# Decay factors of a Mamba-2 scan made once per row and spread from device memory; last stores on two queues

## Chip, cores and metric

The kernel runs on one core of a Trainium2 chip. The metric is the device time of one launch in microseconds (us). Engines: PE (matrix products), DVE (vector), ACT (scalar, activation), POOL (general, elementwise here), SP (here only a queue that issues transfers). SP's and ACT's queues both issue DMA transfers.

## What is computed

A state-space scan (Mamba-2) over 4 batches, 8 heads, 768 steps, head width 32, state width 16, and then a two-layer network with a PReLU between.

```python
log_a = np.log(np.clip(a, 1e-06, 1.0))
for c in range(nc):                      # chunks of the sequence
    cum = np.cumsum(log_a[:, :, sl], axis=-1)
    L = np.exp(cum[:, :, :, None] - cum[:, :, None, :]) * causal
    y_intra = einsum('bhij,bhjd->bhid', einsum('bhin,bhjn->bhij', Cc, Bc) * L, xc)
    y_inter = einsum('bhin,bhnd->bhid', Cc, state) * np.exp(cum)[:, :, :, None]
    y[:, :, sl] = y_intra + y_inter
    state = exp(sum(la)) * state + sum_j Bc[j] xc[j] * exp(cum[-1] - cum[j])
x = y.transpose(0, 2, 1, 3).reshape(3072, 256)
h = x @ w_in                             # 256 x 2048
g = np.maximum(h, 0) + alpha * np.minimum(h, 0)
out = g @ w_out                          # 2048 x 256
```

The result does not depend on the length of a chunk. The kernel takes chunks of 128 steps instead of 32, and products of the factors instead of exponentials of sums of logarithms.

## The kernel before

**Pairs.** The sequence has 24 chunks of 128 steps, 6 to a batch. Two chunks form a pair, so there are pairs 0 to 11. `load_pair` issues a pair's transfers on SP: `ap`, the decay factors `a` of 8 heads, each on 16 partitions; `nat`, the rows of B and C; `xt`, the rows of x; and from pair 2 on two tiles `abc` of 128 x 1024, in which every partition holds the factors of all 8 heads of one chunk. For pairs 0 and 1 PE spreads the factors instead (`spread`).

**One pair's work** (`pair`, a generator that is advanced in stages). `pair_loads` clamps both `abc` on POOL (L295) to 1e-6 ... 1, puts 0 at the first step of each head (L297), and then makes `bn` (L302): the rows of B times the decay from their step to the chunk's end. That decay, `prt`, comes from `rows_scan`, a backward scan over 96 rows (2 batches x 8 heads x 6 chunks) on DVE (L269 to L273), and from `rows_turn`, which transposes it on PE (L281). `rows_scan` is made for batches 0 and 1 at pair 0 and for batches 2 and 3 at pair 6. DVE clamps `ap` (L359) and scans it forward into `pf` (L362, two scans of 128), the decay from the chunk's start. `pf` scales C to `cd` (L384) and the old state (L406). `decays` scans `abc` against a repeated identity into `dec`, the matrix L (L340, 128 x 1024; L345 for pairs 0 and 1). PE makes B's product with x (L397, from `bn`), the Gram matrix (L422), and from `dec` the output y (L436, L443), which ACT copies to `xT`.

**The network.** `hidden` multiplies `xT` by a piece of w_in (L465); ACT and DVE apply the PReLU (L468, L469; DVE's result is `gt`). The first 512 tokens go through it in halves of 256 and through `output` (L478) while the weights arrive. Weights come in 16 pieces of 512 KB (`raw`, L171), of 64-bit floats that ACT, POOL and DVE convert (L187 to L218). Afterwards come five groups of 512 tokens, with `hidden_sums` (L513: four subtractions on POOL per 256 hidden units), `products` (L528: seven products in place of eight), `combine` and `finish`, which transposes two tiles on DVE (L559) and stores each in four transfers (L562). `weight_sums` (L501) on POOL runs during the first of these groups.

**Order.** It is written out by hand: the program's order on each engine is the order of the calls, each engine works through its own list, and a semaphore holds an instruction until its inputs are there. Each engine and each queue is strictly in order, SP's too: a transfer that waits for its buffer holds the ones behind it. `abc` has three buffers, so a pair's second `abc` load waits on SP until the pair before has ended its first scan. Transfers take turns on eight semaphores, so each also waits for the eighth before it.

Of the kernel before, what the change touches and what calls it, by code (L numbers as in the profile page):

```python
# [12 lines left out]
ALU = mybir.AluOpType  # L13
# [9 lines left out]
def kernel(  # L23
# [62 lines left out]
    xtp = ctx.enter_context(tc.tile_pool(name="xtp", bufs=2))  # L86
    gp = ctx.enter_context(tc.tile_pool(name="gp", bufs=16))
    op = ctx.enter_context(tc.tile_pool(name="op", bufs=2))
    ps_s = ctx.enter_context(tc.tile_pool(name="ps_s", bufs=2, space=PSUM))
    ps_h = ctx.enter_context(tc.tile_pool(name="ps_h", bufs=2, space=PSUM))  # L90
    ps_q = ctx.enter_context(tc.tile_pool(name="ps_q", bufs=1, space=PSUM))
# [18 lines left out]
    def load_rows(i):  # L110
# [2 lines left out]
        nc.sync.dma_start(out=rows, in_=a.rearrange("b h (c t) -> (b h c) t", t=Q)[i * RW : (i + 1) * RW])  # L113
        loads["r", i] = rows

    def load_pair(gp):

        b, c = divmod(2 * gp, CPB)
        sl = slice(c * Q, (c + 2) * Q)
        nat = ldx.tile([P, 2, 2, H * N], F32, name="nat")  # L120
        xt = ldx.tile([P, 2, HD], F32, name="xt")
        ap = ldx.tile([P, 2 * Q], F32, name="ap")
        first = a[b, 0:1, sl]
        nc.sync.dma_start(out=ap, in_=bass.AP(tensor=first.tensor, offset=first.offset,
                                              ap=[[S, H], [0, N], [1, 2 * Q]]))
# [12 lines left out]
        for k in range(2 if gp >= NB else 0):  # L138
            t = lda.tile([P, H * Q], F32, name="abc")
            first = a[b, 0:1, slice((c + k) * Q, (c + k + 1) * Q)]  # L140
            nc.sync.dma_start(
                out=t.rearrange("p (h t) -> p h t", h=H),
                in_=bass.AP(tensor=first.tensor, offset=first.offset, ap=[[0, P], [S, H], [1, Q]]),
            )
            abc.append(t)
        loads["p", gp] = nat, abc, xt, ap

# [114 lines left out]
    masked = {}  # L262
    prt = {}

    def rows_scan(i):
# [7 lines left out]
        nc.vector.tensor_tensor_scan(out=pr[:, ::-1], data0=d0[:, 1:][:, ::-1],  # L273
                                     data1=ends[:RW, ::-1], initial=0.0,
                                     op0=ALU.mult, op1=ALU.add)
        return pr

    def rows_turn(i, pr):

        ps = ss_tile()  # L280
        nc.tensor.transpose(ps[:, :RW], pr, ident[:RW, :RW])  # L281
        if i == 0:
            nc.tensor.transpose(ps[:, RW : RW + NF], al_n, ident[:NF, :NF])
        t = bat.tile([P, RW], F32, name="prt")
        nc.scalar.copy(out=t, in_=ps[:, :RW])
        if i == 0:
            nc.scalar.copy(out=alpha, in_=ps[:, RW : RW + NF])
        prt[i] = t

    def pair_loads(gp):  # L290

        b, c = divmod(2 * gp, CPB)
        nat, abc, xt, ap = loads["p", gp]
        for t in abc:
            nc.gpsimd.tensor_scalar(out=t, in0=t, scalar1=1.0, scalar2=1e-6,  # L295
                                    op0=ALU.min, op1=ALU.max)
            nc.gpsimd.memset(t[:, ::Q], 0.0)  # L297

        bn = work.tile([P, 2, H * N], F32, name="bn")
        i, bi = divmod(b, 2)  # L300
        pj = prt[i].rearrange("p (b h c) -> p b c h", b=2, h=H)[:, bi, c : c + 2]
        nc.gpsimd.tensor_tensor(  # L302
            out=bn.rearrange("p k (h n) -> p k h n", h=H),
            in0=nat[:, 0].rearrange("p k (h n) -> p k h n", h=H),
            in1=pj.unsqueeze(3).to_broadcast([P, 2, H, N]), op=ALU.mult)
        return bn
# [22 lines left out]
    def pair(gp):  # L329
# [21 lines left out]
        if gp == 0:  # L351
            ahead[0] = spread(z, 0)
            rows_turn(0, rows_scan(0))
        elif gp == 6:
            rows_turn(1, rows_scan(1))
        bn = pair_loads(gp)

        pf = work.tile([P, 2 * Q], F32, name="pf")
        nc.vector.tensor_scalar(out=ap, in0=ap, scalar1=1e-6, scalar2=1.0, op0=ALU.max, op1=ALU.min)  # L359
        for k in range(2):  # L360
            ks = slice(k * Q, (k + 1) * Q)
            nc.vector.tensor_tensor_scan(out=pf[:, ks], data0=ap[:, ks], data1=zeros, initial=1.0,  # L362
                                         op0=ALU.mult, op1=ALU.add)
        if gp == 0:
            decays(0)

# [188 lines left out]
    def finish(g):  # L555

        for i, c in enumerate(ends_of.pop(g)):
            o = op.tile([P, GT], F32, name="o_sb")
            nc.vector.transpose(o, c.rearrange("p h t -> p (h t)"))  # L559
            for a4 in range(P // 32):  # L560
                m0 = i * HM + 32 * a4
                nc.sync.dma_start(  # L562
                    out=out[g * GT : (g + 1) * GT, m0 : m0 + 32].rearrange("(b r) c -> r b c", r=32),
                    in_=o[32 * a4 : 32 * a4 + 32].rearrange("r (b c) -> r b c", c=32))

# [26 lines left out]
    for n in range(2):  # L592
        for f in range(NF):
            i = (n * NF + f) // 2
            if (n, f) in ((0, 9), (1, 1), (1, 9)):
                load_pair({(0, 9): 2, (1, 1): 3, (1, 9): 4}[n, f])
            if f in (first, second)[n]:
                ssm(*(first, second)[n][f])
            if f % 2 == 0 and i + 2 < len(pieces):
                convert_a(*pieces[i + 2])  # L600
            hidden(0, f, n * 2 * Q, 2 * Q)
            if f % 2 == 0:
                if i + 6 < len(pieces):
# [8 lines left out]
    for i in range(NQ * (NG - 1) + LAG):  # L612
        g, q = divmod(NQ + i, NQ)
        nxt = 2 * g + 2 + q // 4
        if q % 4 == 0 and nxt < NP:
            if nxt == 4:
                load_rows(1)
            if nxt + 1 < NP:
                load_pair(nxt + 1)
        if i < NQ:  # L620
# [47 lines left out]
```

## Time and profile before

| | |
|---|---|
| median of 3 runs | 435.44 us (435.26 to 435.72) |
| profiled execution, whole | 437.33 us |
| its span, first to last instruction | 435.6 us |
| mean granted PE clock | 0.978 |
| busy: PE, DVE, ACT, POOL | 402.2, 237.6, 123.2, 246.7 us |
| POOL clamps L295 | 20 of 1658 ns, 33.2 us |
| DVE scans L362 | 24 of 772 ns, 17.6 us |
| DVE clamps L359 | 12 of 524 ns, 6.3 us |

Times are from the profiled execution. A row of a timeline reads: start in us, length in us, engine, line, operation, output and inputs, shapes, and in brackets how long the engine had stood idle before and what released it. "x4" are four such instructions. A row of the chain of waits has only start, length, engine, tile and line. "PEclk" or the granted clock is the share of full speed that PE had. The stages: start to about 107 us (weights arrive, pairs 0 to 3 are scanned, the first 512 tokens), then the loop over five groups of 512 tokens to about 420 us, two pairs to a group, then the end.

### The profile page before, as it was taken

To read this page: it belongs to the slowest core of one execution; us is meant where nothing else is said; L and a number is where in the kernel's file an instruction comes from. 1 tells how busy PE (TensorE), PEld (TensorE's weight loads), DVE (VectorE), ACT (ScalarE), POOL (GpSimd) and SP (SyncE) were. 2 spreads that over 40 slices of the span, in tenths; PEclk is the share of its full clock that TensorE was granted. 3 is DMA by queue.
4 is the path that set the end of the run, shared out by engine and by line. 5 is a ranking of instruction groups with operands and counts; after the bars stand their busy time and mean duration, and the time that the engine had idled before them with its cause. 6 is when DMAs were issued, how large, how long until landed. Compare 5 with 4: busy or idle time off the path is not lost.

```text
span 435.6 us, 5196 instructions
## 1 busy us (share of the span) xinstructions
PE 402.2 (92%) x1851; PEld 262.9 (60%) x1851; DVE 237.6 (55%) x347; ACT 123.2 (28%) x236; POOL 246.7 (57%) x306
## 2 busy tenths in 40 slices
PE   5877699999999798999899899899899899999992
PEld 4564548778566455656557557556557556666671
DVE  5999796772834633954832853842853842252223
ACT  3554713523223111313212312312312312131210
POOL 2345676371786955953943953953953942453441
PEclk9998969999999899999999999999999999999997
DMA  9949775250530610105730105730102000002002
GB/s 217 233 159 203 229 187 96 70 93 0 132 74 1 123 35 0 50 1 88 155 73 2 48 0 85 157 74 2 48 1 50 0 0 2 0 8 43 0 0 48
DMA packets 123609, 30.32 MB, mean 70 GB/s; under 512 B 96752, under 2 KB 119488, under 8 KB 123584
## 3 DMA queue, kind: packets, MB, share of 16 engines
q1 hardware_dynamic: 119424, 29.74, 30.4%
q10 hardware_dynamic: 4160, 0.26, 0.6%
q8 instruction: 14, 0.23, 0.2%
q14 instruction: 11, 0.09, 0.1%
HBM read 26.85 MB, written 3.15 MB: 69 GB/s over the span
## 4 chain that ended last, share of the span: by engine, by line
PE 76%; POOL 13%; DVE 7%; issue 1%; DMA 1%; ACT 1%; DVEq 0%; POOLq 0%; ACTq 0%
PE hp L465 32%; PE bank L528 23%; PE bank L478 6%; POOL abc L295 6%; PE ss L422 5%; POOL gt L513 3%; PE ss L443 2%; PE ss L436 2%; PE ss L397 2%; DVE dec L345 2%; DVE wr L215 1%; POOL bn L302 1%; PE ss L371 1%; DVE gt L469 1%; DMA ap<-in_a_dram 1%
## 5 line engine op out<-in xcount | busy, mean ns | idle before, releaser
L513 POOL TENSOR_TENSOR gt<-gt 128x256 f32<-128x256 f32 x160 | 134.6, 854 | 128.7 <-DVE gt L469 109.7
L465 PE MATMUL hp<-xT,w_in 128*128 128x512 f32 (+1 forms) x416 | 182.2, 561 | 2.3 <-DVE gt L469 2.3
L469 DVE SCALAR_TENSOR_TENSOR gt<-hp,s_mul,gt 128x512 f32<-128x512 f32 (+1 forms) x104 | 71.4, 687 | 147.6 <-ACT gt L468 147.1
L468 ACT ACTIVATE gt<-hp,s_alpha 128x512 f32<-128x512 f32 (+1 forms) x104 | 66.6, 641 | 233.4 <-PE hp L465 204.0
L465 PEld LDWEIGHTS hp<-xT,w_in 128*128 128x128 f32 x416 | 77.2, 194 | 65.4 <-issue 53.7
L528 PEld LDWEIGHTS bank<-gt,w_out 128*128 128x128 f32 x320 | 61.0, 191 | 41.2 <-issue 36.7
L528 PE MATMUL bank<-gt,w_out 128*128 128x256 f32 x320 | 82.2, 379 | 0.0
L528 PE MATMUL bank<-gt,ws 128*128 128x256 f32 x240 | 64.9, 379 | 0.0
L340 DVE TENSOR_TENSOR_SCAN dec<-abc,ident_h 128x1024 f32<-128x1024 f32 x20 | 50.4, 2518 | 4.5 <-POOL abc L297 4.5
L528 PEld LDWEIGHTS bank<-gt,ws 128*128 128x128 f32 x240 | 45.6, 190 | 6.2
L295 POOL TENSOR_SCALAR abc<-abc 128x1024 f32<-128x1024 f32 x20 | 33.2, 1658 | 1.6
L427 DVE TENSOR_TENSOR dec<-ss,dec 128x512 f32<-128x512 f32 x40 | 25.8, 683 | 12.0 <-PE ss L422 12.0
L478 PE MATMUL bank<-w_out,gt 128*128 128x256 f32 x128 | 30.2, 379 | 0.0
L478 PEld LDWEIGHTS bank<-w_out,gt 128*128 128x128 f32 x128 | 24.3, 190 | 4.2 <-issue 1.0
L422 PE MATMUL ss<-cz,bh 64*128 64x512 f32 x80 | 26.8, 666 | 0.0
L218 POOL TENSOR_TENSOR w_out<-wr,wg 128x512 uint32<-128x512 uint32 x8 | 13.9, 1733 | 12.5 <-DVE wr L215 11.1
L397 PE MATMUL ss<-xt,bn 128*128 128x256 f32 x34 | 10.7, 434 | 9.3 <-POOL bn L302 8.4
L411 POOL TENSOR_TENSOR sm<-state,bmask 128x512 f32<-128x512 f32 (+1 forms) x12 | 13.1, 1088 | 11.0 <-DVE state L406 11.0
L362 DVE TENSOR_TENSOR_SCAN pf<-ap,zeros 128x128 f32<-128x128 f32 x24 | 17.6, 772 | 0.5
L218 POOL TENSOR_TENSOR w_in<-wr,wg 128x512 uint32<-128x512 uint32 x7 | 8.9, 1270 | 12.6 <-DVE wr L215 12.6
L378 ACT ACTIVATE cz<-ss,par 128x256 f32<-128x256 f32 x40 | 15.8, 484 | 0.0
L397 PEld LDWEIGHTS ss<-xt,bn 128*128 128x128 f32 x34 | 6.3, 205 | 12.7 <-POOL bn L302 10.8
(98 smaller groups left out, 288.4 us busy)
## 6 DMA issues: line engine op xcount, KB each, us to landing
abc<-in_a_dram SPq DMA_DIRECT2D x20, 512.0 KB, 5.3
raw<-in_moe_w_in_dram SPq DMA_DIRECT2D x8, 512.0 KB, 5.8
raw<-in_moe_w_out_dram SPq DMA_DIRECT2D x8, 512.0 KB, 5.2
xt<-in_x_dram SPq DMA_DIRECT2D x24, 128.0 KB, 2.9
out_dram<-o_sb SPq DMA_DIRECT2D x40, 64.0 KB, 1.9
ap<-in_a_dram SPq DMA_DIRECT2D x12, 128.0 KB
nat<-in_B_dram SPq DMA_DIRECT2D x22, 64.0 KB, 3.1
nat<-in_C_dram SPq DMA_DIRECT2D x22, 64.0 KB, 2.7
```

The lines of the kernel that those rows point to most:

```text
L218: add.tensor_tensor(out=d, in0=r, in1=g.bitcast(U32), op=ALU.add)
L295: nc.gpsimd.tensor_scalar(out=t, in0=t, scalar1=1.0, scalar2=1e-6, op0=ALU.min, op1=ALU.max)
L340: nc.vector.tensor_tensor_scan(out=dv[:, k], data0=abc[k], data1=ident_h, initial=0.0, op0=ALU.mult, op1=ALU.add)
L397: nc.tensor.matmul(dps[:, k * HD : (k + 1) * HD], bn[:, k], xt[:, k], start=True, stop=True)
L422: nc.tensor.matmul(gram[r].rearrange("p h t -> p (h t)"), bh[rs, k], cz[rs, :, k], start=True, stop=True, tile_position=(64 * r, 0), skip_ ...
L427: nc.vector.tensor_tensor(out=dec[:, k, hs], in0=gram[r], in1=dec[:, k, hs], op=ALU.mult)
L465: nc.tensor.matmul(hp, w_in[:, k, f * P : (f + 1) * P], xts[g][:, k, t0 : t0 + nt], start=(k == 0), stop=(k == KC - 1))
L468: nc.scalar.mul(gt, hp, s_alpha[:, f : f + 1])
L469: nc.vector.scalar_tensor_tensor(out=gt, in0=hp, scalar=s_mul[:, f : f + 1], in1=gt, op0=ALU.mult, op1=ALU.max)
L478: nc.tensor.matmul(pos[0][t // 2][:, t % 2], gt[:, t * Q : (t + 1) * Q], w_out[:, f], start=(f == 0 and t % 2 == 0), stop=(f == NF - 1), s ...
L513: nc.gpsimd.tensor_tensor(out=o, in0=x0, in1=x1, op=ALU.subtract)
L528: nc.tensor.matmul(ms[g][i][:, h], w, b, start=(q == 0 and h == 0), stop=(q == NQ - 1), skip_group_check=True)
```

## The change

It has three parts.

1. A new step `rows_out` takes the clamped factors that `rows_scan` has made, scans them forward (`rpf`, 96 x 128), puts 0 at each row's first step, and stores both arrays (`z`: clamped with the zeros; `pf`: the running products) in device memory, on SP. `rows_out(0)` stands in the first pass over the hidden units at f = 3; `rows_scan(1)` and `rows_out(1)` stand at the start of pair 4 (the first scan's result is kept in `held` until pair 6 transposes it).
2. From pair 2 on, `load_pair` fills `abc` from `z` and `ap` from `pf`, in the same shapes and strides as from `a`. The clamps and memsets of `abc` on POOL and the clamp and two scans of `ap` on DVE are gone for these pairs.
3. Of the very last eight stores, every second is issued by ACT's queue instead of SP's.

```diff
@@ load_pair
+        if gp < NB:
+            first = a[b, 0:1, c * Q : (c + 2) * Q]
+            nc.sync.dma_start(out=ap, in_=bass.AP(tensor=first.tensor, offset=first.offset,
+                                                  ap=[[S, H], [0, N], [1, 2 * Q]]))
+        else:
+            rows = scratch["pf", b // 2].rearrange("(b h c) t -> b h (c t)", b=2, h=H)
+            rows = rows[b % 2, :, c * Q : (c + 2) * Q]
+            nc.sync.dma_start(out=ap, in_=rows.unsqueeze(1).to_broadcast([H, N, 2 * Q]))
...
-            first = a[b, 0:1, slice((c + k) * Q, (c + k + 1) * Q)]
-            nc.sync.dma_start(
-                out=t.rearrange("p (h t) -> p h t", h=H),
-                in_=bass.AP(tensor=first.tensor, offset=first.offset, ap=[[0, P], [S, H], [1, Q]]),
-            )
+            rows = scratch["z", b // 2].rearrange("(b h c) t -> b c h t", b=2, h=H)[b % 2, c + k]
+            nc.sync.dma_start(out=t.rearrange("p (h t) -> p h t", h=H),
+                              in_=rows.unsqueeze(0).to_broadcast([P, H, Q]))
@@ rows_scan, rows_out
+        held[i] = d0
         return pr
+
+    def rows_out(i):
+        d0 = held.pop(i)[:, :Q]
+        rpf = prep.tile([RW, Q], F32, name="rpf")
+        nc.vector.tensor_tensor_scan(out=rpf, data0=d0, data1=zeros[:RW], initial=1.0,
+                                     op0=ALU.mult, op1=ALU.add)
+        nc.vector.memset(d0[:, :1], 0.0)
+        for key, t in (("z", d0), ("pf", rpf)):
+            scratch[key, i] = dr.tile([RW, Q], F32, name=f"{key}{i}")
+            nc.sync.dma_start(out=scratch[key, i], in_=t)
@@ pair_loads
-        for t in abc:
-            nc.gpsimd.tensor_scalar(out=t, in0=t, scalar1=1.0, scalar2=1e-6,
-                                    op0=ALU.min, op1=ALU.max)
-            nc.gpsimd.memset(t[:, ::Q], 0.0)
@@ pair
         elif gp == 6:
-            rows_turn(1, rows_scan(1))
+            rows_turn(1, held["pr"])
         bn = pair_loads(gp)
-        pf = work.tile([P, 2 * Q], F32, name="pf")
...
+        pf = ap
+        if not abc:
+            pf = work.tile([P, 2 * Q], F32, name="pf")
...
@@ finish
-                nc.sync.dma_start(
+                eng = nc.scalar if g == NG - 1 and a4 % 2 else nc.sync
+                eng.dma_start(
@@ the order of the calls
+            if (n, f) == (0, 3):
+                rows_out(0)
...
                 load_rows(1)
+                held["pr"] = rows_scan(1)
+                rows_out(1)
```

How it moves instructions, at three places. Line numbers are those of each program. First POOL at the start of pair 5, before and then changed (`gt<-gt` are the subtractions of `hidden_sums`, `ws` and `w_out` the weight sums):

```order
L513 TENSOR_TENSOR gt<-gt 128x256 x4
L501 TENSOR_TENSOR ws_956<-w_out 128x128
L501 TENSOR_TENSOR ws_957<-ws_956,w_out 128x128
L501 TENSOR_TENSOR ws_958<-w_out,ws_957 128x128
L501 TENSOR_TENSOR w_out<-w_out 128x128
L295 TENSOR_SCALAR abc<-abc 128x1024
L297 MEMSET abc 128x8
L295 TENSOR_SCALAR abc<-abc 128x1024
L297 MEMSET abc 128x8
L302 TENSOR_TENSOR bn<-nat,prt 128x256
L513 TENSOR_TENSOR gt<-gt 128x256 x4
```

```order
L533 TENSOR_TENSOR gt<-gt 128x256 x4
L521 TENSOR_TENSOR ws_961<-w_out 128x128
L521 TENSOR_TENSOR ws_962<-ws_961,w_out 128x128
L521 TENSOR_TENSOR ws_963<-w_out,ws_962 128x128
L521 TENSOR_TENSOR w_out<-w_out 128x128
L319 TENSOR_TENSOR bn<-nat,prt 128x256
L533 TENSOR_TENSOR gt<-gt 128x256 x4
```

Four instructions ahead of `bn` are gone; at pairs 7 to 11 the same four stand right behind the subtractions.

Then DVE in the first pass, around f = 3 (`wr` is a weight piece being converted, `dec<-ss` and `dec<-bank` are pair 1's decay scans):

```order
L469 SCALAR_TENSOR_TENSOR gt<-bank,s_mul,gt 128x256
L210 TENSOR_SCALAR wr<-raw 128x512
L215 SCALAR_TENSOR_TENSOR wr<-wt,wr 128x512
L469 SCALAR_TENSOR_TENSOR gt<-hp,s_mul,gt 128x256
L345 SCALAR_TENSOR_TENSOR dec<-ss,ident_h 128x512 x2
```

```order
L489 SCALAR_TENSOR_TENSOR gt<-bank,s_mul,gt 128x256
L216 TENSOR_SCALAR wr<-raw 128x512
L221 SCALAR_TENSOR_TENSOR wr<-wt,wr 128x512
L292 SCALAR_TENSOR_TENSOR rpf<-r_178,zeros 96x128
L294 MEMSET r_178 96x1
L489 SCALAR_TENSOR_TENSOR gt<-hp,s_mul,gt 128x256
L362 SCALAR_TENSOR_TENSOR dec<-ss,ident_h 128x512 x2
```

The row scan and a memset stand between a weight conversion and the next PReLU step. Last SP's queue from the weight loads to pair 2's loads:

```order
L171 DMA raw<-in_moe_w_in_dram 128x2x512 x5
L171 DMA raw<-in_moe_w_out_dram 128x2x512 x3
L124 DMA ap<-in_a_dram 128x1x256
L134 DMA nat<-in_B_dram 128x8x16
L134 DMA nat<-in_C_dram 128x8x16
```

```order
L177 DMA raw<-in_moe_w_in_dram 128x2x512 x5
L297 DMA z_354<-r_178 96x128
L297 DMA pf_356<-rpf 96x128
L177 DMA raw<-in_moe_w_out_dram 128x2x512 x3
L133 DMA ap<-pf_356 128x1x256
L142 DMA nat<-in_B_dram 128x8x16
L142 DMA nat<-in_C_dram 128x8x16
```

The two new stores wait for that row scan and stand ahead of three weight loads and of all of pair 2's loads. The stores of the second half stand in the same way ahead of pair 5's loads.

More of the change, by code (lines that the diff above doesn't have):

```diff
@@ L88 @@
     op = ctx.enter_context(tc.tile_pool(name="op", bufs=2))
+    dr = ctx.enter_context(tc.tile_pool(name="dr", bufs=1, space=bass.MemoryType.DRAM))
     ps_s = ctx.enter_context(tc.tile_pool(name="ps_s", bufs=2, space=PSUM))
@@ L114, in load_rows @@
         loads["r", i] = rows
+    scratch = {}
     def load_pair(gp):
         b, c = divmod(2 * gp, CPB)
-        sl = slice(c * Q, (c + 2) * Q)
         nat = ldx.tile([P, 2, 2, H * N], F32, name="nat")
@@ L122, in load_pair @@
         ap = ldx.tile([P, 2 * Q], F32, name="ap")
-        first = a[b, 0:1, sl]
-        nc.sync.dma_start(out=ap, in_=bass.AP(tensor=first.tensor, offset=first.offset,
-                                              ap=[[S, H], [0, N], [1, 2 * Q]]))
+        if gp < NB:
[6 more added lines that the diff above has]
+            nc.sync.dma_start(out=ap, in_=rows.unsqueeze(1).to_broadcast([H, N, 2 * Q]))
         if gp == 0:
@@ L263 @@
     prt = {}
+    held = {}
     def rows_scan(i):
@@ L354, in pair @@
         elif gp == 6:
-            rows_turn(1, rows_scan(1))
+            rows_turn(1, held["pr"])
         bn = pair_loads(gp)
-        pf = work.tile([P, 2 * Q], F32, name="pf")
[L359 to L363, printed above, removed]
+        pf = ap
+        if not abc:
+            pf = work.tile([P, 2 * Q], F32, name="pf")
+            nc.vector.tensor_scalar(out=ap, in0=ap, scalar1=1e-6, scalar2=1.0, op0=ALU.max,
+                                    op1=ALU.min)
+            for k in range(2):
+                ks = slice(k * Q, (k + 1) * Q)
+                nc.vector.tensor_tensor_scan(out=pf[:, ks], data0=ap[:, ks], data1=zeros,
+                                             initial=1.0, op0=ALU.mult, op1=ALU.add)
         if gp == 0:
```

## The prediction

> **What bounds the kernel now.** I read the page's shares first, then the chain that ended last, then PE's own waits.
>
> ```profile
> span 435.6 us, 5196 instructions
> PE 402.2 (92%) x1851; PEld 262.9 (60%) x1851; DVE 237.6 (55%) x347; ACT 123.2 (28%) x236; POOL 246.7 (57%) x306
> PE 76%; POOL 13%; DVE 7%; issue 1%; DMA 1%; ACT 1%; DVEq 0%; POOLq 0%; ACTq 0%
> PE ss L397 <- POOL bn L302: 8.4, 6, 2.9
> PE bank L397 <- POOL bn L302: 3.3, 1, 3.3
> PE ss L281 <- DVE pr L273: 1.5, 1, 1.5
> ```
>
> The last three rows are PE's waits (total, times, longest). PE is 92% busy, so nothing can be won where it runs and only its 33.4 us of holes can. A 13% share of POOL in the chain does not mean 13% of the time: PE works on beside most of it. The waits say what counts: 11.7 us for `bn` (L302), the small product that POOL makes at each pair's start, and 1.5 us for the row scan L273. The rest is start and end. By pair, from one transpose L371 to the next (pairs 5, 6 and 7; us, then PE, PEld, DVE, ACT, POOL busy, granted clock, DMA share, GB/s):
>
> ```profile
> 135.99:173.98 37.99, 33.56 (x145) 20.23 (x143) 17.86 (x24) 7.86 (x14) 27.28 (x40) 0.96 0.22 46
> 173.98:205.29 31.31, 31.31 (x141) 19.67 (x141) 19.02 (x26) 8.97 (x18) 19.64 (x23) 1.00 0.20 41
> 205.29:238.39 33.10, 32.00 (x145) 20.01 (x144) 16.75 (x21) 7.93 (x14) 19.64 (x22) 1.00 0.43 81
> ```
>
> Pair 6 has no hole at all (31.31 of 31.31). Pair 7 has one of 1.10 us; pair 5 has 4.43 us and a lower clock. DVE and POOL are far from full. So in the main loop PE sets the time, but for one late instruction per pair.
>
> **The main loop: pairs 7 to 11.** One pair's start, first on POOL, then on PE and in the chain:
>
> ```profile
> 208.23 1.04 POOL L295 TENSOR_SCALAR abc<-abc 128x1024 f32<-128x1024 f32 x1
> 209.52 3.08 POOL L295 TENSOR_SCALAR abc<-abc 128x1024 f32<-128x1024 f32 x1
> 212.75 0.64 POOL L302 TENSOR_TENSOR bn<-nat,prt 128x256 f32<-128x256 f32 x1
> 213.45 1.13 PE L397 MATMUL ss<-xt,bn 128*128 128x256 f32 x4 [1.10 <-POOL bn L302]
> 80.86 0.86 PE bank L397 x4
> 209.47 2.29 DVE L340 TENSOR_TENSOR_SCAN dec<-abc,ident_h 128x1024 f32<-128x1024 f32 x1
> ```
>
> The two clamps L295 and their memsets stand in front of `bn`: from 208.23 to 212.75, 4.5 us. PE arrives at 213.45 - 1.10 = 212.35. Without the clamps `bn` runs from 208.2 to 208.9, 3.5 us early. Its next holder would be the subtractions L513 ahead of the clamps, and they end when the first clamp starts, at 208.2, whatever is removed. So each 1.10 goes: 1.10 + 4 x 1.10 of the pairs that follow (8.4 = 2.9 + 5 x 1.1) = **5.5 us**. The products right behind a hole also run slower (1.13 for four against 0.86 where none was awaited): 0.27 in the three pairs with four of them, **0.8 us**. Bounds of this term: 0 if something else holds `bn`, 6.3 in full; I take it in full, since the pair 6 row shows the loop without a hole.
>
> **Pair 5** is worse, because weight sums (L501) also stand ahead:
>
> ```profile
> 139.13 0.75 DVE L469 SCALAR_TENSOR_TENSOR gt<-hp,s_mul,gt 128x512 f32<-128x512 f32 x1 [0.20 <-ACT gt L468]
> 140.22 0.45 POOL L501 TENSOR_TENSOR w_out<-w_out 128x128 f32<-128x128 f32 x1
> 142.05 3.08 POOL L295 TENSOR_SCALAR abc<-abc 128x1024 f32<-128x1024 f32 x1
> 145.98 0.48 PE L397 MATMUL ss<-xt,bn 128*128 128x256 f32 x1 [2.93 <-POOL bn L302]
> 146.68 3.39 PE hp L465 x4
> 107.04 1.72 PE hp L465 x4
> ```
>
> PE arrives at 143.05 and waits 2.93; then four hidden products take 3.39 instead of 1.72, at half clock: 1.67 more. Without the clamps `bn` could run at 140.7, but the scan L340, which today waits for its clamp, can then start as soon as the DVE step of 139.13 ends, about 139.85. The rows show what a POOL instruction suffers beside a scan: the clamp takes 1.04 alone and 3.08 beside the 2.29 us scan. So the last L501 (140.22) waits until about 142.5, `bn` ends at 143.6, and 0.6 us of the hole stays. [...] I take 2.93 - 0.6 = **2.3** for the hole (2.9 if POOL comes first) and **1.7** for the clock, since no drop is seen after holes of 1.5 and less.
>
> **Pair 6.** The rows scan of the second half is now made at pair 4's start, 65 us before the transpose L281 wants it: **1.5 us** (0 if another wait replaces it; the transpose's other input is a constant). At pair 4 it adds DVE work of about 1.3 us where the scans of `ap` (0.74) and their clamp leave, ahead of a step that waits 2.07 us for ACT today. Nothing for that:
>
> ```profile
> 106.14 0.74 DVE L362 TENSOR_TENSOR_SCAN pf<-ap,zeros 128x128 f32<-128x128 f32 x2
> 108.95 0.42 DVE L384 TENSOR_TENSOR cd<-ss,pf 128x256 f32<-128x256 f32 x1 [2.07 <-ACT cz L378]
> 83.57 0.58 SPq L113 DMA_DIRECT2D rows<-in_a_dram  x1
> ```
>
> The rows are issued at 83.57, 22 us ahead, so DVE doesn't wait. On SP the two new stores wait for DVE (about 107) and hold pair 5's loads from 84 to 108; those are wanted at 136. The other L359 and L362 on DVE, up to 2.8 us a pair, lie beside a busy PE and cost or bring nothing there.
>
> **Start: pair 2.** Here DVE sets the pace.
>
> ```profile
> 50.20 1.27 DVE L359 TENSOR_SCALAR ap<-ap 128x256 f32<-128x256 f32 x1
> 51.51 1.53 DVE L362 TENSOR_TENSOR_SCAN pf<-ap,zeros 128x128 f32<-128x128 f32 x2
> 51.13 0.51 ACT L468 ACTIVATE gt<-bank,s_alpha 128x256 f32<-128x256 f32 x1
> 51.85 0.70 ACT L187 ACTIVATE wt<-raw 128x512 f32<-128x512 f32 x1
> 54.83 0.61 POOL L189 TENSOR_SCALAR wt<-wt 128x512 f32<-128x512 f32 x1
> 55.47 0.69 DVE L215 SCALAR_TENSOR_TENSOR wr<-wt,wr 128x512 uint32<-128x512 uint32 x1 [0.58 <-POOL wt L189]
> 56.61 0.79 PE L465 MATMUL hp<-xT,w_in 128*128 128x256 f32 x1 [0.60 <-DVE gt L469]
> 54.80:66.00 11.20, 10.60 (x30) 6.01 (x31) 10.51 (x15) 2.07 (x4) 8.69 (x6) 0.71 0.78 186
> 66.00:107.00 41.00, 41.00 (x251) 34.13 (x250) 25.29 (x44) 13.89 (x29) 19.61 (x25) 1.00 0.34 67
> ```
>
> Without L359 and L362, DVE's next `gt` waits for ACT until 51.13 + 0.51 = 51.64. POOL's L189 waits for ACT's L187, 52.55, and ends at 53.2; L215 then ends at 53.9, the `gt` behind it at 54.3, and PE's product comes at 54.35 instead of 56.61: 2.3 us. From there DVE is back to back (10.51 of 11.20 busy), so at most its 2.8 us of dropped work moves on, and the half clock of that stretch (0.71 in the mean) is mostly covered by DVE. From 66 PE is full and keeps what it has. I take **2.5** (0 if a late load takes its place, 3.5 if PE also profits from the clock: 2.8 and the 0.7 that DVE was idle).
>
> **Start: what is added.** A row scan and a memset on DVE, at about 28.3:
>
> ```profile
> 172.80 0.91 DVE L273 TENSOR_TENSOR_SCAN pr<-r,ends 96x128 f32<-96x128 f32 x1
> 5.30 0.42 DVE L273 TENSOR_TENSOR_SCAN pr<-r,ends 96x128 f32<-96x128 f32 x1
> 21.71 10.44 SPq L171 DMA_DIRECT2D raw<-in_moe_w_out_dram  x3
> 38.31 1.33 SPq L141 DMA_DIRECT2D abc<-in_a_dram  x2
> abc<-in_a_dram SPq DMA_DIRECT2D x20, 512.0 KB, 5.3
> ```
>
> The nearest rows are the same shape's 0.42 and 0.91 (beside POOL); with a 0.06 memset I charge **0.5** (0.3 to 1.0), all on the path, for DVE runs without a gap here. On SP the stores of both rows wait for it (about 29) and hold the first of the three weight loads by some 8 us, from 21.71; the last of the three goes out at 32.2 today, so little of it is passed on. Pair 2's `abc` is read from 54.3 on. Even if all 8 us reached it (issued at 38.3, 5.3 us to land), it would be there at 52. Nothing, at worst 2.
>
> **The end.** Eight stores, now four on SP and four on ACT:
>
> ```profile
> 429.03 4.11 SPq L562 DMA_DIRECT2D out_dram<-o_sb  x8
> 430.00:434.00 4.00, 0.00 (x0) 0.00 (x0) 0.00 (x0) 0.00 (x0) 0.00 (x0) 0.50 0.72 124
> ```
>
> By issue time alone half of 4.11 goes, 2.05. But the DMA engines are 72% busy for the 4 us, so the bytes need 2.9: **1.1 us**, between 0 and 2.05. [...]
>
> **Sum.** 5.5 + 0.8 + 2.3 + 1.7 + 1.5 = 11.8 in the loop, 2.5 - 0.5 = 2.0 at the start, 1.1 at the end: 14.9. The profiled execution took 437.33 (1.7 around its span) and would take 422.4; the median of the three runs is 1.9 lower, 435.44, and gives **420.5 us**.
>
> **Rivals.**
> *The stall stays in part* (12%): POOL is behind `bn` as well, subtractions against scans, and a scan that comes first holds `bn` in the five later pairs too. For: 3.08 against 1.04. Against: `bn` is done at 208.9, a scan can't start before about 209.4. If 0.8 a pair stays, 4 us: 424.5.
> *Loads at the start come late* (8%): SP's 8 us reach pair 2. For: DMA share 0.78 there. Against: the 52 above. The 2.5 goes and 1.5 is added: 424.5.
> *More at the start* (5%): PE gets the half clock back as well, and the stores halve: 1.0 + 0.95 more, 418.5.
> *It doesn't do what it says* (3%): not the clamps but a load or `prt` released `bn`. Then 5.5 + 0.8 + 2.3 + 1.7 stay: 430.8. The POOL rows are back to back, against it.
> *Slower* (3%): reads of the small scratch are slower than those of `a`. Each pair's second `abc` load is issued when the pair before ends its first scan, some 31 us ahead of its own use; 5.3 us to land leave room, and it decides from 31. At 34 us, 3 us in each of ten pairs, 30 - 14.9: 450. Against: strides and sizes are the same as now.
>
> **How the numbers follow.** The forecast has 69%, with its terms' bounds 417.5 to 423. With the two rivals at 424.5 the range is 417 to 424.8, which leaves out the last two and some of the others' edges. Faster by over 0.2% (0.9 us, about what can be told from no change): 95%; within 0.2%: 2%; slower: 3%.
>
> **What will show it.** No L295 on POOL; PE without waits for `bn` but about 0.6 at pair 5, no half clock there; pairs 7 to 11 at 31.3 to 31.8 us; L281 without a wait; the first product behind pair 2's `bn` 2 us earlier; the last stores over about 3 us. A wait of PE for `abc` through DVE, or `bn` behind L513, would make the prediction wrong.

## The result and the profile after

The change takes 419.04 us in the median (418.57 to 419.21, 4 runs), the kernel before, beside it on the same chip, 435.58 us (435.26 to 436.84). The ratio is 0.961, with a 95% interval from 0.959 to 0.963: 16.5 us faster, where 14.9 were forecast. Run again later beside the experiments it took 421.05 us against 437.09, a ratio of 0.963 (0.960 to 0.965).

The profile's page of the changed kernel, its span, the busy time by engine and the shares of the chain of waits:

```profile
span 417.5 us, 5120 instructions
PE 396.6 (95%) x1851; PEld 260.8 (62%) x1851; DVE 215.8 (52%) x321; ACT 123.1 (29%) x236; POOL 220.7 (53%) x266
PE 87%; DVE 6%; POOL 3%; ACT 1%; DMA 1%; issue 1%; DVEq 0%; POOLq 0%
```

POOL loses 26 us of work and DVE 22. POOL's share of the chain falls from 13% to 3%, and nearly all of it goes to PE. Of the 11.7 us that PE waited for `bn`, 0.5 is left, and the 1.5 us for the row scan are gone; three of the waits that remain (total, times, longest), all at the start:

```profile
PE hp L485 <- DVE gt L489: 3.0, 3, 1.3
PE bank L485 <- POOL w_in L224: 2.2, 1, 2.2
PE bank L417 <- POOL bn L319: 0.5, 1, 0.5
```

L319, L417 and L485 are the former L302, L397 and L465. Pairs 5, 6 and 7 of the changed kernel, transpose to transpose, with the columns as before (us, PE, PEld, DVE, ACT, POOL busy, granted clock, DMA share, GB/s):

```profile
132.17:163.97 31.80, 31.66 (x145) 19.71 (x143) 14.47 (x17) 7.86 (x14) 23.51 (x34) 1.00 0.27 54
163.97:195.26 31.29, 31.29 (x142) 19.65 (x141) 16.65 (x24) 8.96 (x18) 18.38 (x20) 1.00 0.20 41
195.26:227.00 31.74, 31.74 (x146) 20.09 (x145) 14.26 (x18) 7.92 (x14) 16.69 (x18) 1.00 0.45 85
```

Pair 5 fell from 37.99 to 31.80, pair 7 from 33.10 to 31.74, and pair 6, which had no hole, stayed. PE has no hole left but 0.14 us at pair 5, and no half clock there.

To see where the 16.5 us are, the program is cut at the same instructions in both: the start from pair 1's to pair 3's transpose, the loop from pair 4's to pair 11's, and from there to the first of the last stores. The kernel before:

```profile
19.89:75.07 55.18, 46.29 (x259) 32.65 (x258) 45.87 (x78) 25.89 (x54) 33.75 (x34) 0.91 0.72 187
106.44:336.81 230.37, 221.55 (x986) 137.20 (x985) 122.93 (x159) 58.67 (x109) 147.07 (x180) 0.99 0.28 57
336.81:429.03 92.22, 89.42 (x347) 58.24 (x345) 34.55 (x50) 20.10 (x34) 46.84 (x61) 1.00 0.04 6
```

The changed kernel:

```profile
19.52:71.25 51.73, 44.37 (x260) 30.85 (x258) 43.48 (x76) 25.91 (x54) 29.64 (x28) 0.97 0.78 200
102.62:321.32 218.70, 218.56 (x986) 137.01 (x985) 107.22 (x139) 58.61 (x109) 131.22 (x156) 1.00 0.33 65
321.32:412.17 90.85, 89.15 (x347) 58.34 (x345) 32.05 (x47) 20.09 (x34) 44.20 (x57) 1.00 0.04 6
```

The loop gives 230.37 - 218.70 = 11.67 us and pair 11 another 1.37: 13.0. Of the 11.67, 8.68 were idle time of PE (8.82 before, 0.14 now) and 2.99 slower products (221.55 us busy before, 218.56 now), half clock among them. That it equals the 11.7 us of PE's waits for `bn` is chance: 3.3 of those belong to pair 2, in the start. The end, from the first of the last stores to the span's end, goes from 435.6 - 429.03 = 6.57 to 417.5 - 412.17 = 5.33: 1.24. The start gives 3.45, but at another clock: 0.97 against 0.91. The second profile of the changed kernel (row below, under the start) had 0.91 as well and shows what the change itself does there: 0.98 us.

### The profile page after: what moved, and what is told of

It is laid out like the page before. It is cut to its first block, busy times and chain, and to the rows that moved or that the text cites. A ratio compares the mean times of both kernels' runs of the same rounds, so it can differ in the third digit from the quotient of the medians.

```text
span 417.5 us, 5120 instructions
## 1 busy us (share of the span) xinstructions
PE 396.6 (95%) x1851; PEld 260.8 (62%) x1851; DVE 215.8 (52%) x321; ACT 123.1 (29%) x236; POOL 220.7 (53%) x266
## 4 chain that ended last, share of the span: by engine, by line
PE 87%; DVE 6%; POOL 3%; ACT 1%; DMA 1%; issue 1%; DVEq 0%; POOLq 0%
PE hp L485 37%; PE bank L548 28%; PE bank L498 7%; PE ss L442 5%; PE ss L463 2%; PE ss L456 2%; DVE dec L362 2%; PE ss L417 1%; PE ss L391 1%; DVE wr L221 1%; PE bank L340 1%; DMA ap<-in_a_dram 1%; PE bank L442 1%; POOL w_in L224 1%; POOL w_out L521 1%
## 5 line engine op out<-in xcount | busy, mean ns | idle before, releaser
L533 POOL TENSOR_TENSOR gt<-gt 128x256 f32<-128x256 f32 x160 | 142.5, 901 | 138.8 <-DVE gt L489 117.1
L485 PE MATMUL hp<-xT,w_in 128*128 128x512 f32 (+1 forms) x416 | 179.1, 553 | 3.0 <-DVE gt L489 3.0
L485 PEld LDWEIGHTS hp<-xT,w_in 128*128 128x128 f32 x416 | 75.8, 190 | 64.8 <-issue 53.1
L357 DVE TENSOR_TENSOR_SCAN dec<-abc,ident_h 128x1024 f32<-128x1024 f32 x20 | 47.9, 2395 | 0.0
L398 ACT ACTIVATE cz<-ss,par 128x256 f32<-128x256 f32 x40 | 15.7, 483 | 0.0
L195 POOL TENSOR_SCALAR wt<-wt 128x512 f32<-128x512 f32 x15 | 11.2, 745 | 6.2 <-ACT wt L193 5.0
L404 DVE TENSOR_TENSOR cd<-ss,ap 128x256 f32<-128x256 f32 x9 | 3.8, 425 | 20.1 <-ACT cz L398 20.1
L442 PEld LDWEIGHTS ss<-cz,bh 64*128 64x128 f32 x80 | 7.4, 191 | 9.1 <-issue 6.4
L469 ACT COPY xT<-ss 128x512 f32<-128x512 f32 x10 | 5.9, 585 | 23.6 <-PE ss L463 23.6
```

The lines of the kernel that those rows point to most:

```text
L357: nc.vector.tensor_tensor_scan(out=dv[:, k], data0=abc[k], data1=ident_h, initial=0.0, op0=ALU.mult, op1=ALU.add)
L398: nc.scalar.mul(cz[:, e].rearrange("p k t -> p (k t)"), ct, par[:, e : e + 1])
L442: nc.tensor.matmul(gram[r].rearrange("p h t -> p (h t)"), bh[rs, k], cz[rs, :, k], start=True, stop=True, tile_position=(64 * r, 0), skip_ ...
L485: nc.tensor.matmul(hp, w_in[:, k, f * P : (f + 1) * P], xts[g][:, k, t0 : t0 + nt], start=(k == 0), stop=(k == KC - 1))
L533: nc.gpsimd.tensor_tensor(out=o, in0=x0, in1=x1, op=ALU.subtract)
```

## Experiments on the loop: place or load

Times of the experiments are medians; the kernel before, run beside each of them, took 436.9 to 437.1 us. Two theories of the 13 us. The forecast's, A: the clamps stood ahead of `bn` in POOL's list, and only their place counts. The rival, B: POOL and DVE have less to do altogether and hold each other less, so that removed work counts wherever it stands.

**Before, with `bn` made ahead of the clamps.** Nothing is removed, POOL's order alone is changed:

```diff
-        for t in abc:
-            (clamp and memset on POOL)
         bn = ...
+        for t in abc:
+            (clamp and memset on POOL)
```

> The kernel before with one edit: on POOL, bn is made ahead of the two clamps of abc instead of behind them; no work is removed, nothing goes through device memory. Theory A (PE's holes come from the place of the clamps ahead of bn): the holes at pairs 5 and 7 to 11 go (5.5 + 0.8 + 2.9 + 1.7 = 10.9), pair 6's 1.5 and the start stay, pair 2 gains nothing because DVE and the weight clamp behind it stay where they were: 424.6. [...]

Measured: 431.38 us (428.51 to 431.62), a ratio of 0.986 (0.983 to 0.988). The window of the loop in this kernel, and that of pair 5:

```profile
104.80:328.85 224.05, 221.33 (x987) 138.21 (x986) 121.88 (x159) 58.61 (x109) 146.95 (x180) 1.00 0.29 58
134.35:169.78 35.43, 32.71 (x145) 20.01 (x143) 17.81 (x24) 7.86 (x14) 27.26 (x40) 1.00 0.24 49
```

6.3 of the 11.7 us came, by order alone. Of the missing 5.35, 1.5 are the row scan of pair 6, which this kernel keeps. Of the other 3.9, pair 5 has 2.1 (35.43 - 31.80 - 1.5), and pairs 7 to 10 between 0.05 and 0.6 each. The timeline of pair 5:

```profile
139.00 0.64 POOL L297 TENSOR_TENSOR bn<-nat,prt 128x256 f32<-128x256 f32 x1
140.97 2.29 DVE L339 TENSOR_TENSOR_SCAN dec<-abc,ident_h 128x1024 f32<-128x1024 f32 x1 [2.73 <-POOL abc L304]
147.56 1.12 PE L421 MATMUL ss<-cz,bh 64*128 64x512 f32 x2 [1.22 <-DVE state L405]
```

`bn` is early, but the decay scan now waits 2.73 us for the clamp that went behind `bn`; with it what follows on DVE is later, the new state L405 too, and the Gram products L421 wait 1.22 us for that. In pairs 7, 8 and 10 the profile shows no wait, but there too the time is lost at L421: measured from the pair's transpose, these products come 0.5 to 0.6 us later than in the change, and the rest of the pair adds nothing to it. So the clamp had two who waited for it: `bn` by its place in the list, the scan by its data. A's expectation for this kernel, 424.6, missed the second, and the measured time lies 6.8 us above it. Whether work as such costs anything is left to the next two.

**The change, with clamps that nobody reads, behind `bn`, and ahead of it.** Both add, in every pair from 2 on, two clamps of a constant tile into a spare tile and their memsets on POOL, as long as the removed ones:

```diff
+        for t in abc:
+            nc.gpsimd.tensor_scalar(out=idle, in0=ident_h, scalar1=1.0, scalar2=1e-6,
+                                    op0=ALU.min, op1=ALU.max)
+            nc.gpsimd.memset(idle[:, ::Q], 0.0)
```

Behind `bn`:

> The change with POOL's old work put back as work that nobody reads: behind bn in every pair from 2 on, two clamps of a constant tile of 128 x 1024 into a spare tile and their memsets (1.04 and 0.11 us alone, as the clamps of abc had). In the kernel before with bn made first, the loop from pair 4's to pair 11's transpose took 224.05 us, in the change 218.70; 1.5 of that is the row scan. Theory A' (the other 3.9 are scans that wait for their clamp, and the state update and Gram products behind them): unread work costs nothing, 218.7 to 219.2. [...]

Measured: 422.51 us (421.81 to 423.37), a ratio of 0.967 (0.965 to 0.970). Its loop, and POOL in pair 7:

```profile
106.55:325.26 218.71, 218.56 (x987) 136.96 (x986) 109.01 (x139) 58.67 (x109) 143.84 (x180) 1.00 0.32 65
```

```profile
201.89 0.65 POOL L320 TENSOR_TENSOR bn<-nat,prt 128x256 f32<-128x256 f32 x1
203.91 2.72 POOL L325 TENSOR_SCALAR idle<-ident_h 128x1024 f32<-128x1024 f32 x1
```

Ahead of `bn`:

> As the last, but the unread clamps stand ahead of bn, where the clamps of abc stood. Theory A (place ahead of bn): the holes at pairs 5 and 7 to 11 come back nearly in full, five of about 1.1 and one of 2 to 3, loop from pair 4 to pair 11 at 227 to 229 against 218.70. The scans now don't wait for the clamps, so each second one may meet two scans and the holes may grow to 3 us a pair, up to 235. Rival (the holes of before came from abc's loads or prt, not from POOL's list): as the last, 219.

Measured: 438.84 us (437.30 to 440.37), a ratio of 1.005 (1.003 to 1.007). Its loop, its wait for `bn`, and POOL and PE in pair 7:

```profile
105.40:339.77 234.37, 224.07 (x987) 138.44 (x986) 108.61 (x139) 58.67 (x109) 145.41 (x180) 0.98 0.31 61
```

```profile
PE ss L422 <- POOL bn L324: 11.0, 7, 4.4
```

```profile
209.91 3.10 POOL L317 TENSOR_SCALAR idle<-ident_h 128x1024 f32<-128x1024 f32 x1
213.17 2.60 POOL L324 TENSOR_TENSOR bn<-nat,prt 128x256 f32<-128x256 f32 x1
215.83 1.63 PE L422 MATMUL ss<-xt,bn 128*128 128x256 f32 x4 [2.96 <-POOL bn L324]
```

The same clamps, 12.6 us of POOL work in the loop (143.84 against 131.22), cost 0.01 us behind `bn` (218.71 against 218.70) and 15.7 us ahead of it. This settles it for POOL's work in the loop: place, not load; DVE's work is tested below. For the kernel above it leaves, by exclusion, the scan that needs its clamp as the cause of the 3.9 us: unread clamps in that place cost nothing. Ahead of `bn` they cost more than the 11.7 us that the change won, though the row scan is not among it. Of the 15.7 us, 11.7 lie in two pairs: pair 5 takes 38.56 us against 31.80 and pair 7 takes 36.65 against 31.74. PE waits there 4.42 and 2.96 us, where it waited 2.93 and 1.10 in the kernel before, and behind these holes PE runs 6.8 and 3.4 us at half clock. In pair 7 the second decay scan (213.06 to 215.34 on DVE), which no longer waits for a clamp, meets `bn` itself, which takes 2.60 us instead of 0.64. In pair 5 it is the last weight sum (2.43 us) and the second clamp (2.72) that meet scans.

Behind `bn` is not free everywhere. At the start a weight conversion stands there, and PE's wait for the step that needs it grew, from 1.3 us at most to 3.7. Its start from pair 1 to pair 3 took 55.38 us, against 54.20 in the second profile of the change with the same 10.2 us of half clock, and the whole time is 1.5 us above the change's second median:

```profile
PE hp L490 <- DVE gt L494: 5.4, 3, 3.7
```

**Half the change: only `abc` from device memory** (its `ap` still comes from `a` and is clamped and scanned on DVE), and **only `ap`** (its `abc` still comes from `a` and is clamped on POOL ahead of `bn`; the stores of `z` are left out).

`abc` alone:

```diff
-        if gp < NB:
+        if True:
             first = a[b, 0:1, c * Q : (c + 2) * Q]
...
-        pf = ap
-        if not abc:
+        if True:
             pf = work.tile([P, 2 * Q], F32, name="pf")
```

> The change without pf: abc comes clamped from device memory (POOL's clamps gone), ap comes from a and is clamped and scanned on DVE in every pair as before; the row scan of the second half is early, the end is on two queues. Theory A: loop 11.8 and end 1.1 as in the change; pair 2 gains only the 0.6 that DVE waited for POOL's weight clamp, no row scan is added at the start: 13.5 faster, 422.0; PE's waits for bn gone. Rival B (DVE's removed scans count in the loop as well): 425 or more.

`ap` alone:

```diff
-            rows = scratch["z", b // 2].rearrange("(b h c) t -> b c h t", b=2, h=H)[b % 2, c + k]
+            first = a[b, 0:1, slice((c + k) * Q, (c + k + 1) * Q)]
...
         nat, abc, xt, ap = loads["p", gp]
+        for t in abc:
+            nc.gpsimd.tensor_scalar(out=t, in0=t, scalar1=1.0, scalar2=1e-6,
+                                    op0=ALU.min, op1=ALU.max)
+            nc.gpsimd.memset(t[:, ::Q], 0.0)
```

> The change without z: ap comes scanned from device memory (DVE's clamps and scans gone, up to 21 us of DVE work), abc comes from a and is clamped on POOL ahead of bn as before; the row scan of the second half is early, the end is on two queues. Theory A: the holes at pairs 5 and 7 to 11 stay; won are 1.5 at pair 6 and 1.1 at the end, lost 0.5 at the start: 2.1 faster, 433.4. Rival B (removed work counts wherever it lies): 5 us faster or more, 430 or less.

Measured: `abc` alone 422.38 us (421.99 to 422.58), a ratio of 0.967 (0.965 to 0.968); `ap` alone 433.47 (432.76 to 435.09), 0.993 (0.991 to 0.995). Both as expected. Start and loop with `abc` alone:

```profile
19.67:74.31 54.64, 46.18 (x259) 32.83 (x258) 45.39 (x80) 25.92 (x54) 29.68 (x28) 0.91 0.74 188
105.68:324.59 218.91, 218.56 (x986) 136.97 (x985) 118.26 (x159) 58.61 (x109) 132.03 (x156) 1.00 0.33 65
```

and with `ap` alone, and this kernel's wait for `bn`:

```profile
19.79:75.12 55.33, 46.19 (x259) 32.70 (x258) 42.72 (x75) 25.86 (x54) 33.60 (x35) 0.91 0.71 180
106.49:335.72 229.23, 221.59 (x986) 137.35 (x985) 110.11 (x138) 58.61 (x109) 146.42 (x180) 0.99 0.31 62
```

```profile
PE ss L422 <- POOL bn L324: 8.6, 7, 2.8
```

In the loop the clamps of `abc`, with the earlier row scan that both halves have, are all but 0.2 us of the gain (218.91); the clamps and scans of `ap`, 11 us of DVE work there (118.26 against 107.22), are worth that 0.2 us. So B is out for DVE's work too. `ap` alone gives 1.1 us in the loop, with the wait for `bn` as it was; the earlier row scan is in that kernel, and the next experiment prices it.

**The row scan of the second half back at pair 6.** `rows_out(1)` stays at pair 4, only the backward scan returns:

```diff
-            rows_turn(1, held["pr"])
+            rows_turn(1, rows_back(1))
...
-                held["pr"] = rows_scan(1)
+                rows_scan(1)
```

> The change, but the second half's backward row scan (not its clamp, not the forward scan) is put back to pair 6's start. Theory A: PE's transpose there waits again for DVE's scan, which takes 0.4 to 0.9 after the PReLU step: 0.7 to 1.1 us slower than the change. Rival (the 1.5 us of pair 6 went for another reason, the removed clamp and scans of ap): no difference.

Measured: 420.58 us (420.38 to 422.11), a ratio of 0.963 (0.961 to 0.965), which can't be told from the change's own spread (418.57 to 422.12 over both its sets). The window of pair 5 and PE's wait can:

```profile
134.04:166.78 32.74, 31.85 (x144) 19.64 (x143) 15.13 (x18) 7.86 (x14) 24.04 (x35) 1.00 0.26 53
```

```profile
PE ss L307 <- DVE pr L287: 0.7, 1, 0.7
```

0.94 us against 31.80, of it 0.7 of wait. The kernel before waited 0.75 us more there. Its timeline accounts for it: the clamp of the rows and a memset stood ahead of the scan (0.26 us), and the scan itself, which started 0.09 us behind POOL's subtractions, took 0.91 us; here it starts ahead of them and takes 0.41.

## Experiments on the end and the start

**All last stores on SP's queue.**

```diff
-                eng = nc.scalar if g == NG - 1 and a4 % 2 else nc.sync
+                eng = nc.sync
```

> The change with all eight last stores back on SP. Theory A (the order of POOL's list sets the loop, the end is bounded by the DMA engines): 1.1 us slower than the change, about 420.2; the last stores again spread over about 4 us at a DMA share near 0.7. Rival (the end is bounded by issue time alone): 2.0 us slower, about 421.1. Rival (hidden): no difference, 419.0.

Measured: 422.06 us (420.42 to 422.33), a ratio of 0.966 (0.964 to 0.968). The issue of its last stores, and its DMA window:

```profile
413.30 4.11 SPq L583 DMA_DIRECT2D out_dram<-o_sb  x8
```

```profile
414.00:418.00 4.00, 0.00 (x0) 0.00 (x0) 0.00 (x0) 0.00 (x0) 0.00 (x0) 0.71 0.68 116
```

The same in the change:

```profile
412.17 1.96 SPq L583 DMA_DIRECT2D out_dram<-o_sb  x4
412.18 2.08 ACTq L583 DMA_DIRECT2D out_dram<-o_sb  x4
```

```profile
413.00:416.00 3.00, 0.00 (x0) 0.00 (x0) 0.00 (x0) 0.00 (x0) 0.00 (x0) 0.84 1.10 175
```

From the first of these stores to the end it is 419.8 - 413.30 = 6.5 us with one queue and 5.33 with two: 1.2. Issue takes 2.0 us less (4.11 against 2.09), but the DMA engines, 68% busy with one queue from 414 to 418 us, are full with two from 413 to 416 (1.10); that they hold the rest is an inference from these shares. The whole time can't carry this: 422.06 would say 3.0 us against the change's first median and 1.0 against its second, and of the two profiles' difference 1.0 stands in the start (its window there took 52.70 against 51.73), where the two programs are alike.

**The change once more, unaltered**, to see how much of a time is chance:

> The change unaltered, for comparison on the same chip: 419.0. If part of the 18.1 us between the two profiles is chance (the half clock after the 2.15 us hole at the start, which the profile of before shows and that of the change does not), the timed difference stays at 16.5 and the granted clock of the runs of before varies more than that of the change.

Measured: 421.05 us (419.24 to 422.12, 5 runs), a ratio of 0.963 (0.960 to 0.965). Start and loop of its profile:

```profile
19.97:74.17 54.20, 46.36 (x260) 32.95 (x258) 43.03 (x76) 25.86 (x54) 29.67 (x28) 0.91 0.72 187
105.54:324.24 218.70, 218.56 (x986) 136.96 (x985) 107.22 (x139) 58.67 (x109) 131.38 (x156) 1.00 0.33 65
```

The runs don't bear out that the clock varies more before the change: the kernel before was granted 0.977 to 0.985 in its nine runs, the change 0.984 to 0.994. The loop repeats to 0.01 us, the start does not: 54.20 against 51.73 for one and the same program, with 0.91 of the clock against 0.97. By the trace's clock records PE ran 10.2 us at half clock in the start of this execution and 3.4 us in the other (why, stands in the last section). So a start is to be compared at one clock: 55.18 before and 54.20 changed, both at 0.91. With that the account closes: 0.98 + 11.67 + 1.37 + 1.24 = 15.3, and the spans differ by 435.6 - 420.4 = 15.2.

**`rows_out(0)` earlier**, right behind pair 0's decays instead of at f = 3, where DVE has no gap:

```diff
         if gp == 0:
             decays(0)
+            rows_out(0)
...
-            if (n, f) == (0, 3):
-                rows_out(0)
```

> The change, but the first half's forward row scan, memset and stores stand right behind pair 0's first decay scans, where DVE waits 1.3 us for PE, instead of at f = 3, where DVE never rests. Theory A (the added scan costs 0.45 us on the path at f = 3, and holding SP costs nothing): 0.45 us faster than the change, 418.6. Rival (SP's hold of 8 us also cost something): 1 us or more faster. Rival (the added scan is hidden in the change): no difference.

Measured: 419.20 us (418.89 to 420.70), a ratio of 0.961 (0.959 to 0.963). Its start, at 0.97, compares with the first profile of the change:

```profile
19.71:70.99 51.28, 44.36 (x260) 31.05 (x259) 43.07 (x74) 25.98 (x54) 29.66 (x28) 0.97 0.78 203
```

51.73 - 51.28 = 0.45 us, the row scan and its memset taken off the path, as expected; the whole time is within the spread.

**The same, and one weight conversion moved.** At 40 us PE waits 2.2 us for POOL (the L485 row among the waits); at f = 6 POOL's clamp of that weight piece now goes ahead of pair 1's mask:

```diff
+            swap = (n, f) == (0, 6)
+            if swap:
+                convert_a(*pieces[i + 2])
             if f in (first, second)[n]:
                 ssm(*(first, second)[n][f])
-            if f % 2 == 0 and i + 2 < len(pieces):
+            if f % 2 == 0 and i + 2 < len(pieces) and not swap:
```

> As the last, and at f = 6 of the first pass the weight piece's clamp stands ahead of pair 1's state mask on POOL instead of behind it; DVE waits 0.5 us for that clamp in the change and a DVE step beside the mask takes 1.32 instead of 0.42. Theory A (the chain there runs mask, clamp, DVE, add, PE): another 0.5 us faster, 418.1; PE's longest wait at the start, 2.15 us, gets 0.5 shorter. Rival (the mask is what counts there and comes later now): no difference or slower.

Measured: 418.64 us (417.81 to 420.15), a ratio of 0.959 (0.956 to 0.961). Its wait at that place and its start:

```profile
PE bank L486 <- POOL w_in L224: 1.7, 1, 1.7
```

```profile
19.69:70.57 50.88, 43.00 (x259) 30.35 (x258) 43.05 (x74) 25.96 (x54) 29.62 (x28) 1.00 0.79 202
```

The hole shrank by 0.5 us and this execution had no half clock in the start. It has the lowest median, 2.4 us below the change run on the same chip, but the intervals of the two ratios touch (0.956 to 0.961, and 0.960 to 0.965). Of the 2.4 us the starts of two profiles account for 0.85 (51.73 - 50.88, with 3.4 us of half clock in the first of them); the rest is probably clock, which no run separates. Whether the shorter hole makes the half clock rarer can't be said from one profile.

## Why the prediction was right, and where it was off

The time lies inside the range both times, and the forecast's mechanism is the one that the runs show. By its own steps:

- **Pairs 7 to 11** (5.5 + 0.8): right in kind, measured 5 x 1.37 = 6.8. Each hole went whole. The slower products behind a hole were counted in three pairs; PE's busy time fell in all five (32.00 to 31.74 in pair 7), which is the missing 0.5.
- **Pair 5** (2.3 + 1.7 + 1.5 = 5.5): measured 37.99 - 31.80 = 6.19. The clock came back, and the row scan's wait went. The 0.6 us of hole that was to stay was 0.14. The place of the changed kernel:

```profile
135.97 2.50 DVE L357 TENSOR_TENSOR_SCAN dec<-abc,ident_h 128x1024 f32<-128x1024 f32 x1
136.28 2.44 POOL L521 TENSOR_TENSOR w_out<-w_out 128x128 f32<-128x128 f32 x1
138.68 0.63 POOL L319 TENSOR_TENSOR bn<-nat,prt 128x256 f32<-128x256 f32 x1
```

  The scan did start without its clamp and did hold the last weight sum, 2.44 us for an instruction of 0.45. But this sum ends 0.25 us behind the scan and `bn` starts there, where the forecast had the sum start only about 0.4 us behind the scan and take its whole 0.45 then. The step that failed is the last addition, 143.6 for the end of `bn`; counted from the transpose it came at 7.14 us instead of 7.61.
- **Pair 6** (1.5, inside pair 5's window): the wait is gone; put back alone it is 0.7 us of wait and 0.94 in the window.
- **The start** (2.5 - 0.5): the added 0.5 was right (0.45). The forecast of the product was right too; the timeline of pair 2 in the changed kernel:

```profile
52.79 1.70 PE L485 MATMUL hp<-xT,w_in 128*128 128x256 f32 x4 [1.34 <-DVE gt L489]
```

  From pair 2's transpose to that product it is 52.79 - 46.08 = 6.71 us, before 56.61 - 47.67 = 8.94: 2.2 us earlier, 2.26 forecast. What failed is the step from there to pair 3, "I take 2.5": at equal clock only 1.0 of a net 2.0 arrives there. The forecast took the half clock of that stretch as mostly covered by DVE. Three executions in which the program of this stretch, from pair 2's to pair 3's transpose, is the same show how far that holds. In order, they are the earlier `rows_out` with the moved weight conversion, the change's first profile and its second, with no half clock in the stretch, 3.4 us and 6.8 us:

```profile
45.39:70.57 25.18, 21.53 (x119) 15.21 (x118) 19.62 (x33) 11.08 (x25) 15.74 (x14) 1.00 0.85 197
46.08:71.25 25.17, 22.89 (x120) 15.70 (x118) 19.63 (x33) 11.04 (x25) 15.70 (x14) 0.93 0.83 185
48.15:74.17 26.02, 23.28 (x120) 16.55 (x118) 19.19 (x33) 11.04 (x25) 14.59 (x13) 0.87 0.72 156
```

  The kernel before took 27.40 us there, with 22.45 us of DVE work and 6.8 us of half clock. So 3.4 us of half clock cost nothing, and then 2.2 of the 2.5 us arrive; 6.8 us cost 0.85, and then 1.4 arrive. With DVE's work smaller, the longer half clock is no longer covered. No run fixed the clock, so this stays a reading of a few executions.
  The forecast also gave the whole 2.5 to the DVE clamps and scans of `ap`. The halves say otherwise: `ap` alone made the start no shorter (55.33 against 55.18, with the added row scan in it), `abc` alone 0.5 shorter. With `ap` alone PE still waits 3.2 us for `bn` at pair 2; with `abc` alone the wait moves on:

```profile
55.43 2.07 PE L481 MATMUL hp<-xT,w_in 128*128 128x256 f32 x4 [2.94 <-DVE gt L485]
```

  Two waits stand one behind the other there, and each half alone leaves a long one.
- **SP's stores held loads** without harm, as forecast: pair 2's `abc` went out at 38.67 instead of 38.31.
- **The end** (1.1): measured 1.2. The DMA engines' 72% was the right thing to reckon by; half of the issue time would have been 2.05.
- **Around it**: 13.04 + 0.98 + 1.24 = 15.3 at equal clock against 14.9 forecast, with 1.2 too little in the loop and 1.0 too much at the start. That the sum came so near is partly luck, for these two errors cancel. The rest of the first 16.5 is clock at the start.
- **The rivals**: "the stall stays in part", "loads come late" and "it doesn't do what it says" did not occur: no `bn` wait in pairs 7 to 11, no DVE wait for `abc`. "Slower" by the scratch's reads did not either. "More at the start" did occur in part: in the first profile PE got most of its half clock back and the start gave 3.45 us, while the stores gave 1.2 and not 2.05. The first median, 419.04, is nearer to this rival's 418.5 than to the forecast's 420.5, the second, 421.05, nearer to the forecast; which of them an execution gives depends on its clock at the start.

## What to carry to other kernels

Before a moved or removed instruction is priced, two lists are needed: who stands behind it on its engine, and who reads what it makes; the same two clamps a pair, 12.6 us of POOL work in the loop, cost nothing in one place and 15.7 us in another, and moving work behind one waiter only helped half because a second one read it. An engine's busy time says little here, and so does the sum of one wait over the whole program, unless it is split by stage: 11 us of DVE work taken out of the loop were worth 0.2. Where a chance clock moves the total by more than the term in question, compare the stretch between the same two instructions, and only at the same granted clock.

## What was not expected of the hardware

- Whether a hole of PE was followed by half clock went, in these traces, by how it fell on a grid. One program spent 3.4 us of its start at half clock in one execution and 10.2 in another, and its start took 51.73 and 54.20 us. In the trace's clock records every change of the clock lies a multiple of 3.41 us from the one before (in the profile of before at 8, 9, 12, 14, 39, 40 and 122 times 3.413 us from the first record), and the grid lies elsewhere in each execution: the first record stands at 13.47 us there and at 12.25 in the changed kernel's first profile. Cut along its own grid, the changed kernel's first profile reads (the hole of 2.15 us at 38 to 40 us, then pair 2's start):

```profile
36.14:39.55 3.41, 2.13 (x9) 0.90 (x8) 2.90 (x5) 1.52 (x3) 2.39 (x3) 1.00 0.78 92
39.55:42.96 3.41, 2.53 (x15) 2.33 (x16) 3.31 (x7) 1.79 (x4) 2.10 (x3) 1.00 0.98 254
...
49.79:53.20 3.41, 1.57 (x7) 0.74 (x6) 3.01 (x6) 2.13 (x5) 2.23 (x4) 1.00 0.94 208
53.20:56.61 3.41, 3.41 (x9) 1.17 (x8) 3.41 (x4) 1.58 (x3) 3.02 (x2) 0.50 1.06 180
```

  and its second profile, at the same hole:

```profile
38.57:41.98 3.41, 1.25 (x7) 0.99 (x6) 3.16 (x7) 1.38 (x2) 2.00 (x3) 1.00 0.95 165
41.98:45.39 3.41, 3.41 (x17) 2.83 (x19) 3.31 (x7) 0.95 (x2) 1.89 (x2) 0.50 1.06 349
```

  In the first the grid cuts the hole in two; each piece leaves PE busy for 2.13 of 3.41 us or more, and the clock stays. In the second the hole lies in one piece, 1.25 us busy, and the next 3.41 us run at half clock. Cut like this from 24 to 27 us on to 171 to 174 us, eight of the profiles (before, both of the change, one queue, `bn` ahead of the clamps, the late row scan, the earlier `rows_out`, the unread clamps ahead of `bn`) say of the pieces at full clock: all nine with PE busy for 0.38 of their time or less were followed by half clock; of the six between 0.44 and 0.48 four were; of the 303 with 0.49 and more none was. So in these profiles the border lies somewhere between 0.38 and 0.49, and it is not sharp. The way back took more: of the pieces at half clock, the 13 with PE busy throughout were followed by full clock, the five with 0.45 to 0.92 by half clock again. By this, pair 2 of the second profile had 6.8 us of half clock, since PE was busy for 3.15 us of the first piece (0.92), and that of the first profile only 3.4, with 3.41 of 3.41. So a hole of 2.16 us was enough in the second profile, and pair 2's 0.50 and 1.34 us in one piece were in the first. The forecast's "no drop is seen after holes of 1.5 and less" was thus too simple; it held at pair 5, where only 0.14 was left.
- In the profile of before and the first of the change, each of the 38 POOL instructions that started during a DVE scan of 128 x 1024 ended only after the scan, 0.25 to 1.07 us behind it, even small ones: the weight sum of the change's pair 5 took 2.44 instead of 0.45 us and ended 0.25 behind the scan. With the unread clamps ahead of `bn`, `bn` took 2.60 instead of 0.64 and ended 0.43 behind it, the clamp 3.10 instead of 1.04 and 0.83 behind it.
- Two queues moved 175 GB/s with the last stores (413 to 416 us in the change) where one moved 116 (the change with one queue) and 124 (before).
